# Softmax sums divided out behind the product with V instead of ahead of it, and the low parts of q and k made on VectorE

## The chip, the cores and the metric

The kernel runs on one core of one Trainium2 chip. The metric is the device time in microseconds (us) from the first to the last instruction of one execution; lower is better. PE is TensorE, DVE is VectorE, ACT is ScalarE, POOL is GpSimd and SP is SyncE, which issues the DMAs here.

## The reference, cut to what matters

```python
def _attn_ref(q, k, v, w1, b1, w2):          # B=2, H=8, S=576, D=64, hidden 32
    scores = scale * np.matmul(q, k.transpose(0, 1, 3, 2))
    x = (psi_rel / psi_i)[..., None]         # log distances, S x S
    h = np.maximum(x @ w1 + b1, 0.0)
    bias = h @ w2
    scores = scores + bias.transpose(2, 0, 1)[None, :, :, :]
    scores = scores - np.max(scores, axis=-1, keepdims=True)
    attn = np.exp(scores)
    attn = attn / (np.sum(attn, axis=-1, keepdims=True) + 1e-09)
    return np.matmul(attn, v)
...
x = attn_out.transpose(0, 2, 1, 3).reshape(B * S, H * D)
x = _moe_ref(x=x, **moe_kwargs)              # 4 experts, 512 -> 1024 -> 512
return _moe2_ref(x=x, **moe2_kwargs)         # 8 experts and a Sinkhorn gate
```

All is float32. Attention is the first fifth of the time, the two expert layers are the rest.

## The kernel before

**Attention** goes over 36 units. A unit is 128 rows of queries (a tile of one batch, or the last 64 rows of both batches together: the first four units), for one pair of heads. The loop `for k in range(U + 3)` is a pipeline written out by hand: each engine runs its instructions in the order in which the loop emits them, and waits for the others where data or a buffer is missing. Iteration k holds, in this order:

- `emit_S(k)`, PE: scores of both heads, 8 products in fp32r (16 in the first four units). q and k are each split into a high part that fp32r holds exactly and a low part: `qa` and `qb` (`prep_q`, L246 and L247), and two halves of `kk` (`k_hi`, L222 or L224, and `k_lo`, L228). Behind the second head's scores follows `emit_tail(k-2)`, a transpose of the last 64 columns of both heads (L391), which uses free columns of the same PSUM tile.
- `emit_max(k)`, DVE, L358: scores plus bias into SBUF (`s`) with the maximum, one instruction a head. Its bias tile `bt` comes through DRAM, from `emit_bias_out`.
- `emit_exp(k)`, ACT, L371: exponentials in place, with row sums into `stat`.
- `emit_T(k-2)`, PE, L401: eight transposes of `s` into the PSUM tiles `tp`, and `emit_evac`, which copies them to SBUF as `at` (L410 on ACT, L408 on DVE).
- `groups(1)`: four products of a small network for the bias table (PE, L294), copied out by ACT (L320) and written to DRAM. `hids(1)`, `hids(1)`, `hids(2)`: the hidden layer of the next group, DVE, L280, in a ring of six places; the last two wait for the group's products. The 36 groups end in iteration 25.
- `emit_recip(k)`: row sums plus 1e-9 (L377) and their reciprocals (L378), on DVE; `emit_norm(k)`: POOL multiplies `s` by them, 128x576 for each head (L383).
- `emit_P(k-3)`, PE, L427: the product of `at` and V into PSUM (`po`), transposed, heads on the partitions and rows of queries along the free dimension; `emit_x(k-3)`, ACT, L439: `po` to SBUF as `rows`.
- For every new tile and pair, `prep_q` two tiles ahead: a cast on DVE, a subtraction on POOL. In iterations 16 to 18 and from 23 on a part of `pieces(1, 0)` as well (operands of the first expert layer: L108 to L115 on DVE, L99 on ACT, L100 on DVE and POOL), and from 28 on parts of the first weights (L161 on ACT, L162 on POOL).

**The experts** follow: PE products in split precision (L651, L730), with DVE, ACT and POOL around them.

Of the kernel before, what the change touches and what calls it, by code (L numbers as in the profile page):

```python
# [9 lines left out]
F32 = mybir.dt.float32  # L10
# [18 lines left out]
# token tiles of 128: tile t of batch b; the last 64 rows of both batches share one  # L29
TILES = [(0, 0), (0, 1), (4, 0), (1, 0), (1, 1), (2, 0), (2, 1), (3, 0), (3, 1)]  # L30
# a chunk of tokens falls into two halves of n tokens: its tiles, n, and the pieces that
# pair the halves: (tile, column) of the first and of the second, width, place in the half
# [4 lines left out]
# Winograd's form of Strassen's product for first layers: operands of the tokens and of the weights  # L37
# [3 lines left out]
# columns of the packed constants  # L41
# [7 lines left out]
def attn_moe_moe(ctx: ExitStack, tc: tile.TileContext, pack, keep, rel, qT, kT, vT, w, out):  # L49
# [27 lines left out]
    # the tokens, 128 to a tile: as rows for sums over experts, or transposed for products  # L77
# [12 lines left out]
    def pieces(layer, c):  # L90
        """Work that makes the operands of a chunk, in parts."""
        n = CHUNKS[c][1]
        for i in XA:
            X[layer, c, i] = xpools[c].tile([128, 2, 2, n], F32R, tag=f"x{c}{i}", name=f"x{layer}{c}{i}")

        def split(i, src, o, w, lo):
            x = X[layer, c, i]
            hi = x[:, 0, :, o:o + w]
            sc.activation(out=hi, in_=src, func=AF.Copy)  # L99
            lo.tensor_tensor(out=x[:, 1, :, o:o + w], in0=src, in1=hi.bitcast(F32), op=ALU.subtract)  # L100

        def piece(k1, c1, k2, c2, w, o):
            h1, h2 = col_tile(k1)[:, :, c1:c1 + w], col_tile(k2)[:, :, c2:c2 + w]
            a11, a12, a21, a22 = h1[:, 0:2], h1[:, 2:4], h2[:, 0:2], h2[:, 2:4]
            t1, t2 = (g1.tile([128, 2, 128], F32, tag=f"t{i}", name=f"t{i}_{layer}{k1}")[:, :, 0:w] for i in range(2))

            def part1(eng, other):
                eng.tensor_tensor(out=t1, in0=a21, in1=a22, op=ALU.add)  # L108
                eng.tensor_tensor(out=a21, in0=a11, in1=a21, op=ALU.subtract)
                eng.tensor_tensor(out=t2, in0=t1, in1=a11, op=ALU.subtract)  # L110
                split("A11", a11, o, w, other)

            def part2(eng, other):
                split("A12", a12, o, w, eng)
                eng.tensor_tensor(out=a12, in0=a12, in1=t2, op=ALU.subtract)  # L115
                split("A22", a22, o, w, other)
                split("S1", t1, o, w, eng)

            def part3(eng, other):
                split("S2", t2, o, w, eng)  # L120
                split("S3", a21, o, w, eng)
                split("S4", a12, o, w, eng)

            return [part1, part2, part3]

        return [piece(*x) for x in CHUNKS[c][2]]

    # ------------------------------------------------------------ weights
# [14 lines left out]
    def split_raw(m, add, lo):  # L143
        """Work that makes a granule of what was loaded, in parts."""
# [8 lines left out]
        # B11, B12, B21, B22 -> B11, T1, B21, B22 and T2, T3, -T4  # L153
# [21 lines left out]
    # ------------------------------------------------------------ attention  # L175
    def attention(moe):
# [73 lines left out]
        def load_bias(t, p):  # L250
            # the second head's last 64 columns come before its others, next to the first head's
# [3 lines left out]
            # row i of the tile, column j: distance j - (i0 + i), kept at S - 1 + j - (i0 + i)  # L255
# [9 lines left out]
        # the space of the first weights serves until they come  # L265
# [62 lines left out]
        scps, sm, at_t, po = {}, {}, {}, {}  # L328
        stat = {}

        def emit_S(u):
            t, p, b = units[u]
            for h in range(2):
# [15 lines left out]
                if h == 1 and 2 <= u and made < NGR:  # L349
                    emit_tail(u - 2, sm[u - 2], o[:, 1, 288:416])  # L350
# [25 lines left out]
        def emit_recip(u):  # L376
            ve.tensor_scalar(stat[u][:, 4:6], stat[u][:, 2:4], 1e-9, None, op0=ALU.add)  # L377
            ve.reciprocal(stat[u][:, 6:8], stat[u][:, 4:6])  # L378

        def emit_norm(u):  # L380
            for h in range(2):
                s = sm[u][:, S * h:S * h + S]
                gp.tensor_tensor(  # L383
                    out=s, in0=s, in1=stat[u][:, 6 + h:7 + h].to_broadcast([128, S]), op=ALU.mult
                )
            stat.pop(u)
# [3 lines left out]
        def emit_tail(u, s, tail):  # L390
            pe.transpose(tail, s[:, 512:640], ident)  # L391
            tps[u, 2] = tail

        def emit_T(u):
            s = sm.pop(u)
            if (u, 2) not in tps:
                emit_tail(u, s, pt.tile([128, 1, 512], F32, tag="bps", name=f"tl{u}", bufs=1)[:, 0, 0:128])
            for h in range(2):
                o = pt.tile([128, 4, 128], F32, tag=f"tp{h}", name=f"tp{u}{h}", bufs=1)
                for j in range(4):  # L400
                    pe.transpose(o[:, j, :], s[:, 640 * h + 128 * j:640 * h + 128 * j + 128], ident)  # L401
                tps[u, h] = o
        def emit_evac(u, h, eng):
            o = tps.pop((u, h))
            shape = [128, 4, 128] if h < 2 else [128, 128]
# [7 lines left out]
        def emit_P(u):  # L413
# [4 lines left out]
            a = [at_t.pop((u, h)) for h in range(3)]  # L418
            for bb in [b] if t < 4 else [0, 1]:
                n = 128 if t < 4 else 64  # L420
                c0, i0 = (128 * bb, 0) if t < 4 else (64 * bb, 64 * bb)
                for j in range(5):
                    for h in range(2):
                        r = slice(0, 128) if j < 4 else slice(64 * h, 64 * h + 64)
                        col = (2 * bb + h) * D
                        rhs = a[h][:, j, i0:i0 + n] if j < 4 else a[2][r, i0:i0 + n]
# [8 lines left out]
        def emit_x(u):  # L435
            t, p, b = units[u]
            if t == 4 or b == 1:
                n = 2 if t < 4 else 1
                sc.activation(  # L439
                    out=rows[t][:, :, 128 * p:128 * p + 128],  # L440
                    in_=po.pop((t, p))[:, 0:128 * n].rearrange("p (b c) -> p b c", b=n),
                    func=AF.Copy,
                )

        # ---- emission
        kq = [(p, b) for p in range(4) for b in range(2)]
        # the clock of the tensor engine rises with work: some ahead of the first data
# [36 lines left out]
        for g in range(FIRST):  # L484
            hids(2, (1,))
            groups(1)
            if g == 0:
                load_k(*kq[2])
                prep_q(*tps_[0], gp)
                prep_k(*kq[0], ve, gp)  # L490
            if g == 1:
                load_k(*kq[3])
                prep_k(*kq[1], ve, gp)
                prep_q(*tps_[1], gp)
            if g == 3:
# [5 lines left out]
                prep_k(*kq[2], sc, gp)  # L501
            if g == 4:
                k_hi(*kq[3], sc)
                k_lo(*kq[3], gp)
# [7 lines left out]
        for k in range(U + 3):  # L512
            first = False
            if k < U:
# [5 lines left out]
                emit_max(k)  # L520
            elif k == U:
                st_sc.close()
# [29 lines left out]
            if k < U:  # L552
                emit_recip(k)
                emit_norm(k)
# [4 lines left out]
            # loads and preparation ahead  # L559
            if first:  # L560
                if ti + 2 < len(tps_):
                    prep_q(*tps_[ti + 2], gp)
# [5 lines left out]
            if k == 0:  # L568
                k_lo(*kq[4], gp)
# [4 lines left out]
            if k == 1:  # L574
                k_hi(*kq[6], sc)
                k_lo(*kq[6], gp)
# [28 lines left out]
    # ------------------------------------------------------------ experts  # L605
    class Moe:
# [25 lines left out]
        def L1(self, n):  # L632
            """Products of step n's first layer, each with what follows it."""
# [83 lines left out]
        def L2(self, n):  # L717
            """Products of step n's second layer, a tile of tokens each."""
# [56 lines left out]
        # ---- between the layers  # L775
# [101 lines left out]
        def prefetch(self, n, lo=None):  # L877
            k = self.next_split
            m = k - SLOTS
            # granule m was used last in step 2 * NP * expert + NP + pair  # L880
# [50 lines left out]
def _layouts(q, k, v, w1, b1, w2, moe_domain_probs, moe_w1, moe_w2, moe2_w_gate, moe2_w1, moe2_w2):  # L931
# [23 lines left out]
    def granules(wa, wb):  # L955
        # quadrants of a pair of first-layer columns: (rows' half, column) 00, 01, 10, 11
# [26 lines left out]
```

## Time and profile before

| what | value |
|---|---|
| median of 3 runs | 1461.72 us (1458.29 to 1463.8) |
| the profiled execution, first to last instruction | 1461.6 us |
| busy share of that span: PE / DVE / ACT / POOL | 94% / 60% / 35% / 34% |
| mean granted clock of PE, of full speed | 0.972 |
| start of the first scores (PE) | 26.1 us |
| last unit's `emit_max` | 262 us |

The span is the time of one execution under the profiler; it stands within the spread of the three runs. A busy share is an average over stages with different limits, so the stages are read one by one.

### The profile page before, as it was taken

The page shows a single profiled execution, that of the slowest core. Times are in us where ns is not written, and L with a number is a line of the kernel's source. Part 1 is how long each engine was busy: PE and PEld are TensorE (multiplying, and loading weights), DVE is VectorE, ACT ScalarE, POOL GpSimd, SP SyncE. Part 2 cuts the span into 40 slices and gives each one's busy share as a digit, 9 for nine tenths or more (in the row PEclk, how much of TensorE's full clock was granted, in tenths as well). Part 3 has the DMA queues.
Part 4 walks back from the last instruction along what each step waited for, and adds up shares of the span by engine and source line. Part 5 has one row for each costly group of instructions (what it writes and reads, how often), then busy time and mean ns, then how long its engine had stood idle before and what let it go on. Part 6 is the DMA issues. An engine that isn't in the chain of part 4 may idle for free.

```text
span 1461.6 us, 22030 instructions
## 1 busy us (share of the span) xinstructions
PE 1378.2 (94%) x8567; PEld 1190.5 (81%) x8567; DVE 870.3 (60%) x1786; ACT 505.5 (35%) x1202; POOL 492.2 (34%) x413
## 2 busy tenths in 40 slices
PE   6788876899999999999998999999999999999998
PEld 3466555778989989888887889899898898988987
DVE  6888888765646547367458356455463554635633
ACT  4466654432313224134323123132241331422311
POOL 3555446332505216024215026053160440612600
PEclk8899999999999999999999999999999999999999
DMA  6845442010201102002001002011020120200110
GB/s 192 261 140 151 116 122 61 30 58 30 87 1 58 58 1 94 23 14 74 30 29 59 29 30 87 1 59 58 1 88 29 41 76 1 87 30 30 58 37 29
DMA packets 38648, 89.88 MB, mean 61 GB/s; under 512 B 8848, under 2 KB 11664, under 8 KB 38544
## 3 DMA queue, kind: packets, MB, share of 16 engines
q1 hardware_dynamic: 38544, 88.48, 19.5%
q8 instruction: 67, 1.10, 0.3%
q14 instruction: 37, 0.30, 0.1%
HBM read 75.22 MB, written 13.25 MB: 61 GB/s over the span
## 4 chain that ended last, share of the span: by engine, by line
PE 77%; DVE 13%; ACT 5%; issue 3%; DMA 2%; SPq 0%; POOL 0%; DVEq 0%
PE y L730 40%; PE B L651 15%; PE C L651 10%; PE A L651 10%; ACT s L371 3%; DVE hids L280 2%; DVE s L358 2%; ACT at L410 1%; DVE qa L246 1%; DVE x10S L100 1%; PE bps L294 1%; DMA kr<-in_kT 1%; DVE t L110 1%; PE sc L340 1%; PE po L427 0%
## 5 line engine op out<-in xcount | busy, mean ns | idle before, releaser
L730 PE MATMUL y<-gb,h 128*128 128x512 f32 x2592 | 720.2, 398 | 0.0
L730 PEld LDWEIGHTS y<-gb,h 128*128 128x128 f32 x2592 | 455.7, 190 | 57.7 <-issue 0.2
L162 POOL TENSOR_TENSOR gb<-rawb,gb 128x512 fp32r<-128x512 f32 x94 | 125.4, 1346 | 645.1 <-ACT gb L161 645.1
L659 DVE TENSOR_TENSOR u<-B,s 128x320 f32<-128x320 f32 (+1 forms) x192 | 87.6, 456 | 311.3 <-PE B L651 311.2
L662 ACT ACTIVATE h<-c 128x320 fp32r<-128x320 f32 (+1 forms) x288 | 119.6, 439 | 402.8 <-DVE c L659 401.7
L665 DVE SCALAR_TENSOR_TENSOR h<-c,h 128x320 fp32r<-128x320 f32 (+1 forms) x288 | 167.4, 598 | 48.5 <-ACT h L662 43.7
L659 DVE TENSOR_TENSOR c<-C,u 128x320 f32<-128x320 f32 (+1 forms) x192 | 87.4, 455 | 63.3 <-PE C L651 59.8
L162 POOL TENSOR_TENSOR ga<-rawa,ga 128x512 fp32r<-128x512 f32 x94 | 121.1, 1306 | 2.8 <-ACT ga L161 2.8
L383 POOL TENSOR_TENSOR s<-s,stat 128x576 f32<-128x576 f32 x72 | 85.0, 1201 | 106.2 <-DVE stat L378 42.0
L162 POOL TENSOR_TENSOR ga<-wt,ga 128x512 fp32r<-128x512 f32 x94 | 105.0, 1135 | 43.6 <-ACT ga L161 26.1
L673 ACT ACTIVATE s<-A 128x320 f32<-128x320 f32 (+1 forms) x96 | 39.4, 411 | 180.8 <-PE A L651 180.7
L659 DVE TENSOR_TENSOR c<-B,s 128x320 f32<-128x320 f32 (+1 forms) x96 | 43.9, 457 | 81.9 <-PE B L651 80.5
L662 ACT ACTIVATE h<-A 128x320 fp32r<-128x320 f32 (+1 forms) x96 | 38.9, 406 | 151.0 <-PE A L651 151.0
L280 DVE TENSOR_SCALAR hids<-T,b1psi 128x528 f32<-128x528 f32 (+17 forms) x137 | 87.4, 672 | 5.7 <-PE bps L294 5.6
L161 ACT ACTIVATE gb<-rawb 128x512 fp32r<-128x512 f32 x96 | 60.0, 626 | 74.4 <-DMA rawb<-in_w 74.4
L371 ACT ACTIVATE s<-s,stat 128x576 f32<-128x576 f32 x72 | 55.4, 770 | 86.2 <-DVE stat L358 86.2
L340 PE MATMUL sc<-kk,qa 128*128 128x288 f32 x160 | 51.5, 340 | 22.6 <-DVE stat L358 17.2
L651 PE MATMUL C<-x20S,ga 128*128 128x320 f32 x384 | 67.4, 311 | 0.0
L651 PE MATMUL A<-x20A,ga 128*128 128x320 f32 x384 | 66.8, 309 | 0.0
L651 PEld LDWEIGHTS C<-x20S,ga 128*128 128x128 f32 x384 | 62.1, 190 | 5.8
L651 PE MATMUL B<-x20S,ga 128*128 128x320 f32 x384 | 66.5, 308 | 0.0
L651 PEld LDWEIGHTS A<-x20A,ga 128*128 128x128 f32 x384 | 61.6, 189 | 5.7
(157 smaller groups left out, 2104.3 us busy)
## 6 DMA issues: line engine op xcount, KB each, us to landing
rawa<-in_w SPq DMA_DIRECT2D x48, 512.0 KB, 4.1
rawb<-in_w SPq DMA_DIRECT2D x48, 512.0 KB, 4.9
bd<-bsts SPq DMA_DIRECT2D x36, 295.5 KB, 3.4
bt<-bd SPq DMA_DIRECT2D x16, 512.0 KB, 4.4
qr<-in_qT SPq DMA_DIRECT2D x20, 256.0 KB, 3.6
kr<-in_kT SPq DMA_DIRECT2D x8, 576.0 KB, 6.2
bt<-bd SPq DMA_DIRECT2D x8, 256.0 KB, 4.8
V<-in_vT SPq DMA_DIRECT2D x4, 512.0 KB, 6.1
```

What stands on the lines that cost most here:

```text
L161: sc.activation(out=z(0), in_=src, func=AF.Copy)
L162: lo.tensor_tensor(out=z(1), in0=src, in1=z(0).bitcast(F32), op=ALU.subtract)
L280: ve.tensor_scalar(x[:, 0:n], T[:, 0:n], b1psi[:, tt:tt + 1], 0.0, op0=ALU.add, op1=ALU.max)
L340: pe.matmul(out=o[:, j, 0:288], lhsT=qq[t, p][:, 2 * bb + h, :], rhs=kk[p, bb][:, h, 288 * j:288 * j + 288], start=n == 0, stop=n == last,)
L371: sc.activation(out=s, in_=s, func=AF.Exp, scale=-1.0, bias=stat[u][:, h:h + 1], accum_out=stat[u][:, 2 + h:3 + h],)
L383: gp.tensor_tensor(out=s, in0=s, in1=stat[u][:, 6 + h:7 + h].to_broadcast([128, S]), op=ALU.mult)
L651: pe.matmul(out=ban[o], lhsT=a, rhs=x[:, z, k, :], start=not more and i == 0, stop=i == 5, skip_group_check=more,)
L659: ve.tensor_tensor(out=t[o], in0=ban[a], in1=t[b], op=ALU.add)
L662: sc.activation(out=h[f][:, 0, half, :], in_=src, func=AF.Relu)
L665: ve.scalar_tensor_tensor(out=h[f][:, 1, half, :], in0=src, scalar=0.0, in1=h[f][:, 0, half, :].bitcast(F32), op0=ALU.max, op1=ALU.subtract,)
L673: sc.activation(out=t["s1"], in_=ban["A"], func=AF.Copy)
L730: pe.matmul(out=self.y[t], lhsT=a, rhs=x, start=g == 0 and f == 0 and i == 0, stop=g == NP - 1 and f == 1 and i == 2,)
```

## The change

Row sums are no longer multiplied into `s` by POOL. The exponentials are transposed and multiplied by V as they are. The addition of 1e-9 moves from DVE to POOL (`emit_recip`), the reciprocal stays on DVE, one iteration later (`emit_recip2(k-1)`, right behind `emit_max(k)`). Since `po` is transposed, its scale is needed along the free dimension: `emit_tail` makes it with one more small product a head, whose stationary operand is the reciprocal column repeated 64 times and whose moving operand is the identity, so that each of the 64 output partitions holds all 128 reciprocals. It lies beside the transposed tail in PSUM, and the tail's copy to SBUF takes both (256 columns in place of 128). `emit_x` becomes a multiplication on DVE, for each unit, of `po` with that copy, in place of a copy on ACT for every two units. The subtractions of `prep_q` and of six of the eight `k_lo` move from POOL to DVE. Comments were taken out as well.

```diff
@@ emit_S @@
-                    emit_tail(u - 2, sm[u - 2], o[:, 1, 288:416])
+                    emit_tail(u - 2, sm[u - 2], o[:, :, 288:416])
@@ -374,27 +374,29 @@
         def emit_recip(u):
-            ve.tensor_scalar(stat[u][:, 4:6], stat[u][:, 2:4], 1e-9, None, op0=ALU.add)
+            gp.tensor_scalar(stat[u][:, 4:6], stat[u][:, 2:4], 1e-9, None, op0=ALU.add)
+
+        def emit_recip2(u):
             ve.reciprocal(stat[u][:, 6:8], stat[u][:, 4:6])
 
-        def emit_norm(u):
+        tps = {}
+
+        def emit_tail(u, s, o):
+
+            pe.transpose(o[:, 1, :], s[:, 512:640], ident)
+            st = stat.pop(u)
             for h in range(2):
-                s = sm[u][:, S * h:S * h + S]
-                gp.tensor_tensor(
-                    out=s, in0=s, in1=stat[u][:, 6 + h:7 + h].to_broadcast([128, S]), op=ALU.mult
+                pe.matmul(
+                    out=o[64 * h:64 * h + 64, 0, :], lhsT=st[:, 6 + h:7 + h].to_broadcast([128, 64]),
+                    rhs=ident, start=True, stop=True,
                 )
-            stat.pop(u)
-
-        tps = {}
-
-        def emit_tail(u, s, tail):
-            pe.transpose(tail, s[:, 512:640], ident)
-            tps[u, 2] = tail
+            tps[u, 2] = o
...
@@ emit_evac @@
-            shape = [128, 4, 128] if h < 2 else [128, 128]
+            shape = [128, 4 if h < 2 else 2, 128]
@@ emit_P @@
+            rc[u] = a[2][:, 0, :]
...
-                        rhs = a[h][:, j, i0:i0 + n] if j < 4 else a[2][r, i0:i0 + n]
+                        rhs = a[h][:, j, i0:i0 + n] if j < 4 else a[2][r, 1, i0:i0 + n]
@@ -434,17 +437,14 @@
         def emit_x(u):
             t, p, b = units[u]
-            if t == 4 or b == 1:
-                n = 2 if t < 4 else 1
-                sc.activation(
-                    out=rows[t][:, :, 128 * p:128 * p + 128],
-                    in_=po.pop((t, p))[:, 0:128 * n].rearrange("p (b c) -> p b c", b=n),
-                    func=AF.Copy,
-                )
+            ve.tensor_tensor(
+                out=rows[t][:, b, 128 * p:128 * p + 128],
+                in0=po[t, p][:, 128 * b:128 * b + 128], in1=rc.pop(u), op=ALU.mult,
+            )
@@ attention, ahead of the loop and in it @@
-                prep_q(*tps_[0], gp)
-                prep_k(*kq[0], ve, gp)
+                prep_q(*tps_[0], ve)
+                prep_k(*kq[0], ve, ve)
...
-                k_lo(*kq[3], gp)
+                k_lo(*kq[3], ve)
...
                 emit_S(k)
                 emit_max(k)
+                if k > 0:
+                    emit_recip2(k - 1)
...
                 emit_recip(k)
-                emit_norm(k)
...
-                    prep_q(*tps_[ti + 2], gp)
+                    prep_q(*tps_[ti + 2], ve)
...
-                k_lo(*kq[4], gp)
+                k_lo(*kq[4], ve)
```

On DVE, one whole iteration of the middle of attention (from one `emit_max` to the next; `s` and `stat` are the unit's scores and sums, `sc` its PSUM tile, `hids` the hidden layer, `qa` the cast of q) stands before as

```order
L358 ISA s_1048,stat_1047<-sc_1036,bt_901 128x576
L358 ISA stat_1047 128x1
L358 ISA s_1048,stat_1047<-sc_1041,bt_901 128x576
L358 ISA stat_1047 128x1
L280 TENSOR_SCALAR hids<-T,b1psi 128x304
L408 COPY at_1076<-sc_1041 128x128
L280 TENSOR_SCALAR hids<-T,b1psi 128x304
L377 TENSOR_SCALAR stat_1047<-stat_1047 128x2
L378 RECIPROCAL stat_1047<-stat_1047 128x2
L280 TENSOR_SCALAR hids<-T,b1psi 128x304 x2
L246 CAST qa_1096<-qr_840 128x512
```

and the same iteration of the changed kernel as

```order
L358 ISA s_1047,stat_1046<-sc_1033,bt_897 128x576
L358 ISA stat_1046 128x1
L358 ISA s_1047,stat_1046<-sc_1038,bt_897 128x576
L358 ISA stat_1046 128x1
L380 RECIPROCAL stat_983<-stat_983 128x2
L280 TENSOR_SCALAR hids<-T,b1psi 128x304
L410 COPY at_1076<-sc_1038 128x256
L280 TENSOR_SCALAR hids<-T,b1psi 128x304 x3
L440 TENSOR_TENSOR rows_76<-po,at_1013 128x128
L246 CAST qa_1093<-qr_835 128x512
L247 TENSOR_TENSOR qb_1094<-qr_835,qa_1093 128x512
```

The addition has gone, the reciprocal is that of the unit before (`stat_983`), and the product of `po` and the subtraction for `qb` are new.

On PE, an early unit of the changed kernel, from its last score product to the first product with V (`kept` holds the identity):

```order
L340 MATMUL sc_617<-kk_160,qb_499 128x288
L386 MATMUL sc_617<-kept,s_450 128x128
L389 MATMUL sc_617<-kept,stat_449 64x128 x2
L403 MATMUL tp_631<-kept,s_450 128x128 x4
L403 MATMUL tp_636<-kept,s_450 128x128 x4
L294 MATMUL bps_644<-hids,w2n 32x416 x4
L430 MATMUL po<-at_547,V_101 64x64
```

The row with `stat_449` is new: two small products between the tail's transpose and the others, which need the reciprocals of the unit two back.

## Rows read from the trace of the kernel before

**Rows 1.** Windows: stretch, length, busy us (instructions) of PE, PEld, DVE, ACT, POOL, clock, DMA.

```profile
72.00:146.00 74.00, 66.30 (x682) 47.27 (x679) 64.65 (x158) 47.65 (x113) 39.96 (x34) 0.95 0.52 149
146.00:216.00 70.00, 54.66 (x457) 38.22 (x459) 61.70 (x137) 40.27 (x105) 34.81 (x32) 0.93 0.44 124
216.00:262.00 46.00, 32.21 (x277) 25.41 (x273) 39.01 (x78) 23.26 (x69) 27.87 (x27) 0.92 0.17 49
```

**Rows 2.** Waits, 84 to 195 us: who waited for whom, us in total, times, longest.

```profile
ACT s L371 <- DVE stat L358: 38.6, 18, 4.1
...
DVE stat L377 <- ACT s L371: 12.0, 19, 0.7
```

**Rows 3.** Timeline near 124 us: start, duration, engine, line, operation, idle before.

```profile
123.74 0.39 DVE L280 TENSOR_SCALAR hids<-T,b1psi 128x336 f32<-128x336 f32 x1
...
125.60 1.59 DVE L280 TENSOR_SCALAR hids<-T,b1psi 128x336 f32<-128x336 f32 x2
125.85 2.34 POOL L383 TENSOR_TENSOR s<-s,stat 128x576 f32<-128x576 f32 x2 [2.03 <-PE tp L401]
```

**Rows 4.** Timeline: two casts of q, and POOL's next instruction beside the second.

```profile
131.84 1.37 DVE L246 CAST qa<-qr 128x512 fp32r<-128x512 f32 x1
...
206.19 0.41 DVE L246 CAST qa<-qr 128x512 fp32r<-128x512 f32 x1
...
206.44 2.31 POOL L383 TENSOR_TENSOR s<-s,stat 128x576 f32<-128x576 f32 x2 [3.74 <-ACT rows L439]
```

**Rows 5.** Groups by line, 0 to 310 us: count, busy us, mean ns, idle before; POOL and DVE.

```profile
L383 POOL TENSOR_TENSOR s<-s,stat 128x576 f32<-128x576 f32 x72 | 85.0, 1201 | 106.2 <-DVE stat L378 42.0 <-ACT rows L439 15.9 <-PE tp L401 15.6
L247 POOL TENSOR_TENSOR qb<-qr,qa 128x512 fp32r<-128x512 f32 x20 | 25.7, 1285 | 12.8 <-DVE qa L246 11.9 <-ACT kk L222 0.4 <-PE tp L401 0.4
...
L228 DVE TENSOR_TENSOR kk<-kr,kk 64x1152 fp32r<-64x1152 f32 x2 | 5.2, 2603 | 0.1
...
L100 DVE TENSOR_TENSOR x10S<-rows,x10S 128x128 fp32r<-128x128 f32 x10 | 9.9, 1025 | 0.0
```

**Rows 6.** Timeline behind attention: a DVE subtraction, and POOL's next instruction.

```profile
273.59 0.68 DVE L162 TENSOR_TENSOR gb<-rawb,gb 128x512 fp32r<-128x512 f32 x1
...
286.38 1.34 POOL L162 TENSOR_TENSOR gb<-rawb,gb 128x512 fp32r<-128x512 f32 x1 [18.68 <-ACT gb L161]
```

**Rows 7.** Timeline: DVE's copies out of PSUM, 128 and 512 columns.

```profile
124.04 0.28 DVE L408 COPY at<-sc 128x128 f32<-128x128 f32 x1
...
204.33 0.68 DVE L408 COPY at<-tp 128x512 f32<-128x512 f32 x1
```

**Rows 8.** Timeline: PE from one unit's scores to the next unit's.

```profile
129.44 0.40 PE L340 MATMUL sc<-kk,qa 128*128 128x288 f32 x1
...
131.48 0.66 PE L401 MATMUL tp<-kept,s 128*128 128x128 f32 x4 [0.18 <-ACT at L410]
...
132.80 1.46 PE L427 MATMUL po<-at,V 128*64 128x128 f32 x20
...
134.19 0.40 PE L340 MATMUL sc<-kk,qa 128*128 128x288 f32 x1
```

**Rows 9.** Groups by line, 0 to 310 us: ACT's exponentials, bias table and copies.

```profile
L371 ACT ACTIVATE s<-s,stat 128x576 f32<-128x576 f32 x72 | 55.4, 770 | 86.2 <-DVE stat L358 86.2
L320 ACT ACTIVATE bsts<-bps,cst 128x64 f32<-128x64 f32 (+35 forms) x72 | 36.2, 502 | 25.6 <-PE bps L294 17.4 <-DMA bd<-bsts 3.7 <-DMA V<-in_vT 3.3
L410 ACT ACTIVATE at<-tp 128x512 f32<-128x512 f32 x59 | 34.3, 582 | 0.5 <-PE tp L401 0.5
```

**Rows 10.** Timeline: first `emit_max` instruction of units 0, 4, 17, 28 and 35.

```profile
32.78 0.76 DVE L358 CUSTOM_DVE_ANT_0 s<-sc,bt 128x576 f32<-128x576 f32 x1 [2.59 <-DMA bt<-bd]
...
71.50 0.76 DVE L358 CUSTOM_DVE_ANT_0 s<-sc,bt 128x576 f32<-128x576 f32 x1 [1.42 <-POOL qb L247]
...
145.87 0.74 DVE L358 CUSTOM_DVE_ANT_0 s<-sc,bt 128x576 f32<-128x576 f32 x1
...
215.93 0.74 DVE L358 CUSTOM_DVE_ANT_0 s<-sc,bt 128x576 f32<-128x576 f32 x1
...
261.99 0.74 DVE L358 CUSTOM_DVE_ANT_0 s<-sc,bt 128x576 f32<-128x576 f32 x1
```

More of the change, by code (lines that the diff above doesn't have):

```diff
@@ L326, in emit_bias_out @@
             )
-        scps, sm, at_t, po = {}, {}, {}, {}
+        scps, sm, at_t, po, rc = {}, {}, {}, {}, {}
         stat = {}
@@ L396, in emit_T @@
             if (u, 2) not in tps:
-                emit_tail(u, s, pt.tile([128, 1, 512], F32, tag="bps", name=f"tl{u}", bufs=1)[:, 0, 0:128])
+                o = pt.tile([128, 1, 512], F32, tag="bps", name=f"tl{u}", bufs=1)
+                emit_tail(u, s, o[:, 0, 0:256].rearrange("p (a c) -> p a c", a=2))
             for h in range(2):
@@ L488, in attention @@
                 load_k(*kq[2])
-                prep_q(*tps_[0], gp)
-                prep_k(*kq[0], ve, gp)
+                prep_q(*tps_[0], ve)
+                prep_k(*kq[0], ve, ve)
             if g == 1:
                 load_k(*kq[3])
-                prep_k(*kq[1], ve, gp)
-                prep_q(*tps_[1], gp)
+                prep_k(*kq[1], ve, ve)
+                prep_q(*tps_[1], ve)
             if g == 3:
@@ L500, in attention @@
                 load_q(*tps_[2])
-                prep_k(*kq[2], sc, gp)
+                prep_k(*kq[2], sc, ve)
             if g == 4:
                 k_hi(*kq[3], sc)
-                k_lo(*kq[3], gp)
+                k_lo(*kq[3], ve)
             if g == 5:
@@ L520, in attention @@
                 emit_max(k)
+                if k > 0:
+                    emit_recip2(k - 1)
             elif k == U:
+                emit_recip2(k - 1)
                 st_sc.close()
@@ L575, in attention @@
                 k_hi(*kq[6], sc)
-                k_lo(*kq[6], gp)
+                k_lo(*kq[6], ve)
                 k_hi(*kq[7], sc)
```

## The prediction

> **What bounds the kernel now.** I read the page first: PE is busy for 94% of the span and its slices are full wherever the experts run. The change touches nothing there, so all it can move lies in attention, which I read by stages. The windows show that DVE, not PE, is the fuller engine in the middle and at the end of attention: 64.65 us of 74, 61.70 of 70 and 39.01 of 46, while PE falls to 54.66 of 70 and 32.21 of 46 [rows 1]. PE leads only in the first of the three, with 66.30.
>
> The waits name the link: ACT stood 38.6 us in 111 for `emit_max` on DVE, and DVE itself stood 12.0 us for the exponentials before it could add 1e-9, in 19 waits [rows 2]. A busy engine is not yet a working one. The timeline shows one `hids` instruction of 336 columns at 0.39 us, and two us later a pair of the same at 1.59, when POOL multiplies `s` [rows 3]. A cast of q takes 1.37 us in one place and 0.41 in another, where POOL had been idle for 3.74 us and starts only after most of the cast [rows 4]. So DVE is slow where POOL runs, and POOL runs the 72 multiplications that are removed, 85.0 us in all [rows 5].
>
> The Trainium skill (SBUF — State Buffer, section "SBUF: two separate sides") calls the ports that DVE and POOL share an exclusive lock, held for a whole instruction. The trace agrees, with 0.39 against about 0.80 a piece for `hids`. By that rule the subtractions that move to DVE cost their undisturbed time; by the disturbed rows [rows 5] the same 26 would be dearer by 20 x 0.61 + 6 x 1.07 = 19 us.
>
> The time per unit, from the starts of `emit_max` [rows 10]: units 4 to 17 take 74.37 us, 5.72 each; 17 to 28 take 70.06, 6.37 each; 28 to 35 take 46.06, 6.58 each.
>
> **The change, part by part.** I make the sum for a middle unit first, on DVE.
> - Removed: the slow half of `hids`, 1.59 - 2 x 0.39 = 0.81 us [rows 3]; in every second unit the slow cast, 1.37 - 0.41 = 0.96, so 0.48 a unit [rows 4]; the wait for the exponentials, 12.0 / 19 = 0.63 [rows 2], since the reciprocal is now taken a whole iteration later, when the sums are long there. The addition's own time goes too; I don't count it.
> - Added: `emit_x`, 128 columns out of PSUM, like the copy of 0.28; the tail's copy with 256 columns, by the two copies of 128 and 512, 0.40 x 128 / 384 = 0.13 more [rows 7]; `qb` in every second unit. With POOL silent (its next instruction comes 13 us later, after 18.68 us of idleness) a subtraction of 512 columns takes 0.68 [rows 6], so 0.34 a unit.
> - DVE would then need 5.72 - 0.81 - 0.48 - 0.63 + 0.28 + 0.13 + 0.34 = 4.55 us a unit.
>
> On PE the fastest unit of before took 134.19 - 129.44 = 4.75 us, of which 0.18 was a wait for ACT [rows 8]. The two products with the reciprocals are not in the trace. The nearest are the products with V: 20 records, two for each of ten products, in 1.46 us, 0.07 a record [rows 8], so four records cost 0.29. Bounds: nothing, if they lie beside others in other columns of the array, and 0.66, what four transposes of as many columns take [rows 8]. I take 0.29, the row they are nearest to: PE needs 4.75 - 0.18 + 0.29 = 4.86. PE takes over from DVE.
>
> A new wait comes with it. `emit_x` on DVE waits for the product with V, which is the last thing PE does in an iteration; the casts, `qb` and the next `emit_max` are queued behind it, and ACT waits for that. Link by link over two units: `emit_x` 0.28, cast 0.41, `qb` 0.68, `emit_max` of two heads 2 x 0.74 [rows 4, 6, 7, 10], then on ACT the second exponential 0.77, two bias copies 1.00 and the second copy 0.58, with the first exponential and first copy, 0.77 + 0.58, partly beside `emit_max` (I count all but the 0.74 of its second head) [rows 9], then on PE the last transposes and bias products 131.48 to 132.80 = 1.32 and the product with V 1.46 [rows 8]. That is 8.59 us, and with nine hand-overs of an estimated 0.15 each 9.9 us for two units, 4.97 each. It binds as tightly as PE does. I take 5.0 us a unit.
>
> The addition on POOL costs nothing: between the sums and the reciprocal lies a whole iteration less `emit_max`, some 3 us. ACT loses the copies of `po`, which it does beside others.
>
> By stages:
> - Units 4 to 17: 13 x 5.0 = 65.0 instead of 74.37, -9.4.
> - Units 17 to 28: seven of the eleven carry a part of `pieces(1, 0)`, three subtractions on DVE, 1.03 us each now [rows 5]; undisturbed they can't be below the 0.28 of a small copy [rows 7]. POOL still makes some low parts there, so I take 0.45 each, 1.35 a unit: DVE needs 4.55 + 1.35 = 5.9 where `hids` still run and less where they have ended; 5.6 on the mean. 7 x 5.6 + 4 x 5.0 = 59.2 instead of 70.06, -10.9.
> - Units 28 to 35: no `hids` and no bias products, but `pieces`, the copy of half of `tp` on DVE (0.68) and the first weights on ACT and POOL. I take 5.2: 36.4 instead of 46.06, -9.7. Bounds of both pieces stages: PE's 4.86, and the 5.9 of DVE.
> - Start to unit 4 (71.5 us): the first `emit_max` waits 2.59 us for the bias tile by DMA [rows 10], so faster `hids` ahead of it help little. Of the six `k_lo` that come to DVE, the ones for the third, fourth and seventh tile need ACT's copy of k, which stands behind the bias copies; the `hids` queued behind them on DVE wait too, and PE's bias products for those. Each costs at most 0.68 x 1152 / 512 = 1.5 us undisturbed [rows 6], where the two already on DVE go from 2.60 [rows 5] to that. Gain and loss nearly meet; the slow `hids` and casts of units 2 and 3 remain. I take -4, between 0 and -8.
> - Behind unit 35: the last transposes no longer wait for POOL's 2.3 us [rows 4]; -1, between 0 and -3.
>
> Sum: -9.4 - 10.9 - 9.7 - 4 - 1 = -35 us. The profiled execution is 1461.6 us, the median of the runs 1461.72, so both lead to **1427 us**.
>
> **The rivals.**
> - *More* (PE alone sets the pace, the loop over `emit_x` is slack, the products with the reciprocals are nearly free): 31 units at 4.86, 150.7 instead of 190.5, -39.8, with -8 and -3 at the ends, -51: 1411 us. For it: PE reached 4.75 even beside POOL. Against it: DVE's 5.9 in the units with pieces. Chance 0.13.
> - *Less* (the loop over `emit_x` binds harder): with hand-overs of 0.30 instead of 0.15 it is 11.3 us, 5.6 a unit, and 6.0 where pieces stand in it: -1.6, -6 and -4, with -2 at the start, -14: 1448 us. For it: every link is in-order and none can be overtaken. Against: the loop spans two units and the fast ones of before had such hand-overs too. Chance 0.19.
> - *Slower*: the slow `hids` and casts are not POOL's doing, and stay. Then DVE, the fuller engine, only gains the 0.63 of the wait and pays 0.28 + 0.13 + 1.29 / 2 = 1.06 (`qb` at its present 1285 ns [rows 5]): +0.43 a unit, 13 us in 31 units, and six `k_lo` at 2.6 us, 15.6, half of them exposed: 1461.6 + 21 = 1483 us. It decides if less than 0.12 us a unit (0.28 + 0.13 + 0.34 - 0.63) of the slowness is POOL's. Against it stand the paired rows [rows 3, 4]. Chance 0.05. The Trainium skill (Perfetto Trace Analysis, section "Optimizing Scalar/DVE Operations") advises moving work off a saturated DVE, to GpSimd too, which is the reverse of this edit; the same passage adds that between these two it might not help, as they share a port, and the pairs above agree with the second half.
> - *No change*, within 7 us, if the DMAs behind the bias tiles (`emit_bias_out` to `load_bias`) hold the units at their present times. Against: after the first units `emit_max` hardly waits for one [rows 10]. Chance 0.03.
>
> **How the numbers follow.** The likeliest case, -26 to -44 us, has 0.60; the predicted time is its middle. A measurement of this kernel tells about 0.5%, 7.3 us, from no change. Faster takes the likeliest, *more* and *less*: 0.92; same 0.03; slower 0.05. The range reaches to *more* and nearly all of *less*: 1411 to 1447. What is left out is about 0.15: the end of *less*, no change, slower, and a sliver beyond *more*.
>
> **What the changed profile would show.** Right: `hids` near 0.4 us a piece instead of 0.67 and casts near 0.41; DVE without a wait for the exponentials, but with one for the product with V at `emit_x`; units 4 to 17 about 5.0 us apart, with PE busy for over 92% there; no unit with pieces above 6; the reciprocals' products near 0.3 us a unit; `qb` on DVE near 0.68; the experts as long as before. Wrong: casts that stay over 1 us although POOL is idle (the port is not the cause); units at 5.5 and more with DVE waiting long at `emit_x` (*less*); a first `emit_max` well behind 33 us (the moved `k_lo` hold the start); reciprocals that wait for POOL's addition.

## The result

The changed kernel takes 1419.43 us (median, 1415.2 to 1420.91) beside 1460.01 us for the kernel before on the same chip: the ratio is 0.9715, with a 95% interval of 0.9693 to 0.9738. The profiled execution spans 1418.1 us, 43.5 less than that of before. The prediction was 1427 us, in a range of 1411 to 1447.

The windows of the changed kernel answer to [rows 1]; the columns are the same.

```profile
72.00:146.00 74.00, 74.00 (x795) 52.54 (x793) 59.95 (x190) 52.48 (x123) 5.00 (x17) 1.00 0.54 154
146.00:216.00 70.00, 68.89 (x665) 49.63 (x662) 60.08 (x182) 51.24 (x137) 13.89 (x26) 1.00 0.48 137
216.00:262.00 46.00, 43.51 (x326) 36.37 (x324) 35.81 (x72) 23.80 (x60) 15.69 (x16) 1.00 0.21 67
```

PE (first busy figure) is now without a gap from 72 to 146 us and nearly so behind; POOL (fifth) fell from 39.96 to 5.00 us in the first of the three stretches of [rows 1]. PE's granted clock is 1.00 where it was 0.92 to 0.95.

The groups by line on DVE and POOL, 0 to 270 us, answer to [rows 5]; columns are count, busy us, mean ns, idle before. `hids` and the cast stood before as

```profile
L280 DVE TENSOR_SCALAR hids<-T,b1psi 128x528 f32<-128x528 f32 (+17 forms) x137 | 87.4, 672 | 5.7 <-PE bps L294 5.6
...
L246 DVE CAST qa<-qr 128x512 fp32r<-128x512 f32 x20 | 20.2, 1010 | 0.3 <-DMA qr<-in_qT 0.3
```

and the changed kernel has

```profile
L280 DVE TENSOR_SCALAR hids<-T,b1psi 128x528 f32<-128x528 f32 (+17 forms) x137 | 53.8, 438 | 2.9 <-PE bps L294 2.5
...
L247 DVE TENSOR_TENSOR qb<-qr,qa 128x512 fp32r<-128x512 f32 x20 | 14.1, 705 | 0.7
L228 DVE TENSOR_TENSOR kk<-kr,kk 64x1152 fp32r<-64x1152 f32 x8 | 10.8, 1355 | 8.6 <-ACT kk L222 8.5
L440 DVE TENSOR_TENSOR rows<-po,at 128x128 f32<-128x128 f32 x36 | 10.4, 289 | 16.3 <-PE po L430 15.5 <-ACT at L412 0.8
L410 DVE COPY at<-sc 128x256 f32<-128x256 f32 x24 | 10.0, 417 | 0.0
...
L246 DVE CAST qa<-qr 128x512 fp32r<-128x512 f32 x20 | 8.4, 418 | 0.0
...
L100 DVE TENSOR_TENSOR x10S<-rows,x10S 128x128 fp32r<-128x128 f32 x10 | 2.4, 284 | 0.0
...
L377 POOL TENSOR_SCALAR stat<-stat 128x2 f32<-128x2 f32 x36 | 11.0, 307 | 189.0 <-ACT s L371 178.1 <-PE bps L294 9.4 <-issue 1.5
```

The durations came out close to the undisturbed rows: the cast 418 ns, `qb` 705, the multiplication at L440 289, the tail's copy 417, and the subtractions of `pieces` fell from 1025 ns to 284. What DVE waits for now stands in the idle columns: 15.5 us for the product with V at L440, and 8.5 us for ACT's copies of k at L228.

The first `emit_max` of units 0, 4, 17, 28 and 35 answers to [rows 10].

```profile
35.39 0.76 DVE L358 CUSTOM_DVE_ANT_0 s<-sc,bt 128x576 f32<-128x576 f32 x1 [2.21 <-PE sc L340]
...
71.38 0.75 DVE L358 CUSTOM_DVE_ANT_0 s<-sc,bt 128x576 f32<-128x576 f32 x1
...
136.82 0.75 DVE L358 CUSTOM_DVE_ANT_0 s<-sc,bt 128x576 f32<-128x576 f32 x1
...
191.36 0.74 DVE L358 CUSTOM_DVE_ANT_0 s<-sc,bt 128x576 f32<-128x576 f32 x1
...
220.92 0.75 DVE L358 CUSTOM_DVE_ANT_0 s<-sc,bt 128x576 f32<-128x576 f32 x1
```

So the 43.5 us fall as follows, by differences of such starts: start to unit 4, 0.1; units 4 to 17, 8.9; 17 to 28, 15.5; 28 to 35, 16.5; behind unit 35, 2.4. Of the last one 1.6 us come and go between executions: the same program takes 1197.2 us behind unit 35 here and 1198.8 in another execution.

### The profile page after: what moved, and what is told of

It is laid out like the page before. It is cut to its first block, busy times and chain, and to the rows that moved or that the text cites. A ratio compares the mean times of both kernels' runs of the same rounds, so it can differ in the third digit from the quotient of the medians.

```text
span 1418.1 us, 22243 instructions
## 1 busy us (share of the span) xinstructions
PE 1373.2 (97%) x8711; PEld 1185.6 (84%) x8711; DVE 820.9 (58%) x1812; ACT 502.5 (35%) x1182; POOL 377.1 (27%) x351
## 4 chain that ended last, share of the span: by engine, by line
PE 88%; DVE 7%; ACT 2%; issue 1%; DMA 1%; SPq 0%; DVEq 0%; ACTq 0%
PE y L732 40%; PE B L653 16%; PE C L653 10%; PE A L653 10%; PE po L430 3%; PE sc L340 3%; PE bps L294 2%; PE tp L403 2%; ACT s L371 1%; PE sc L389 1%; DVE wt L157 0%; DMA kr<-in_kT 0%; ACT at L412 0%; DVE kk L228 0%; DVE h L667 0%
## 5 line engine op out<-in xcount | busy, mean ns | idle before, releaser
L161 ACT ACTIVATE gb<-rawb 128x512 fp32r<-128x512 f32 x96 | 60.0, 626 | 70.4 <-DMA rawb<-in_w 70.4
L653 PEld LDWEIGHTS B<-x20S,ga 128*128 128x128 f32 x384 | 61.4, 188 | 5.7
L294 PE MATMUL bps<-hids,w2n 128*32 128x264 f32 (+17 forms) x352 | 45.1, 538 | 21.4 <-DVE hids L280 17.4
L377 POOL TENSOR_SCALAR stat<-stat 128x2 f32<-128x2 f32 x36 | 11.0, 307 | 189.0 <-ACT s L371 178.1
```

The lines of the kernel that those rows point to most:

```text
L161: sc.activation(out=z(0), in_=src, func=AF.Copy)
L294: pe.matmul(out=o[32 * q:32 * q + 32, j, 0:n], lhsT=w2n, rhs=hid[g, q][:, n * j:n * j + n], start=True, stop=True,)
L653: pe.matmul(out=ban[o], lhsT=a, rhs=x[:, z, k, :], start=not more and i == 0, stop=i == 5, skip_group_check=more,)
```

## The experiments

The table has the same starts for every run, from its profiled execution (us), and the time per unit in the three stages. Each ratio is against the kernel before on the same chip. The start differs from one execution to the next: unit 4 came at 71.4 and 70.7 us in two executions of the changed kernel, and at 69.3 and 68.8 in two versions (`emit_x` later, products twice) that have the same low parts there and take nothing away from the first units. So differences of up to some 2.6 us at unit 4 show nothing by themselves.

| run | median | ratio, 95% interval | unit 0 | unit 4 | unit 35 | 4 to 17 | 17 to 28 | 28 to 35 |
|---|---|---|---|---|---|---|---|---|
| before | 1460 to 1463 | 1 | 32.8 | 71.5 | 262.0 | 5.72 | 6.37 | 6.58 |
| changed | 1419.4 | 0.9715, 0.9693 to 0.9738 | 35.4 | 71.4 | 220.9 | 5.03 | 4.96 | 4.22 |
| low parts only | 1468.3 | 1.0051, 1.0036 to 1.0065 | 37.0 | 75.0 | 270.5 | 5.95 | 6.42 | 6.79 |
| sums only | 1426.3 | 0.9764, 0.9746 to 0.9782 | 32.5 | 68.2 | 223.5 | 5.10 | 5.05 | 4.77 |
| k's low parts on POOL | 1417.7 | 0.9707, 0.9690 to 0.9725 | 33.2 | 69.3 | 218.9 | 5.03 | 4.96 | 4.22 |
| POOL beside | 1442.9 | 0.9878, 0.9860 to 0.9897 | 35.9 | 73.8 | 241.9 | 5.25 | 5.92 | 4.96 |
| `emit_x` later | 1418.1 | 0.9696, 0.9675 to 0.9718 | 35.1 | 69.3 | 219.3 | 5.01 | 4.95 | 4.34 |
| products twice | 1420.1 | 0.9717, 0.9692 to 0.9741 | 36.4 | 68.8 | 223.4 | 5.25 | 5.11 | 4.31 |
| one product, by DVE | 1420.2 | 0.9712, 0.9689 to 0.9735 | 34.6 | 70.1 | 220.1 | 4.76 | 5.05 | 4.64 |
| k's low parts later | 1418.4 | 0.9701, 0.9681 to 0.9721 | 31.1 | 68.5 | 218.1 | 5.04 | 4.96 | 4.22 |
| changed, again | 1420.9 | 0.9706, 0.9679 to 0.9732 | 35.8 | 70.7 | 220.2 | 5.03 | 4.96 | 4.22 |
| POOL as before | 1442.8 | 0.9868, 0.9846 to 0.9891 | 32.0 | 70.4 | 241.7 | 5.23 | 5.96 | 5.39 |
| reciprocal at once | 1424.8 | 0.9759, 0.9733 to 0.9785 | 36.7 | 73.0 | 230.4 | 5.03 | 5.07 | 5.18 |
| one product by POOL, k later | 1409.1 | 0.9643, 0.9619 to 0.9666 | 31.2 | 68.4 | 213.4 | 4.75 | 4.88 | 4.22 |

**Low parts only.** The kernel before, with this alone:

```diff
-                prep_q(*tps_[0], gp)
-                prep_k(*kq[0], ve, gp)
+                prep_q(*tps_[0], ve)
+                prep_k(*kq[0], ve, ve)
...
-                    prep_q(*tps_[ti + 2], gp)
+                    prep_q(*tps_[ti + 2], ve)
```

> The kernel before with one part of the change alone: the low parts of q and of six tiles of k on VectorE; POOL still multiplies the exponentials by the reciprocals. Theory (POOL's instructions stretch DVE's, and taking the 72 multiplications off POOL is what frees DVE): DVE gets 0.34 us a unit more and loses only the disturbance by the low parts; hids and the cast stay slow beside the multiplications. 1462 to 1475 us, no gain; units 4 to 17 at 5.6 to 6.0 us. Rival (the gain comes from the low parts leaving POOL): most of the 42 us are here already, 1425 to 1435 us.

1468.3 us, 0.5% slower: the rival fell. `hids` stayed slow at 607 ns and the cast at 1080. Unit 35 comes 8.5 us later than before; 3.5 of these are there at unit 4, so a part of the loss lies in the start, where DVE now waits 7.9 us for ACT's copies of k (L228).

**Sums only.** The changed kernel with those lines as they were before.

> The changed kernel with all low parts of q and k back on POOL, so only the row sums are handled anew. Theory: POOL runs 1.3 us in every second unit, beside a cast or hids; DVE then needs about 4.7 us a unit and PE's 4.8 still sets the pace, so the middle stays as in the changed kernel; the first emit_max comes at about 32 us instead of 35.4, since no subtraction on DVE waits for ACT there. 1413 to 1421 us. Rival (the moved low parts carry a part of the gain): 1428 us or more, with units 4 to 17 over 5.3 us.

1426.3 us, between the two expectations: the low parts are worth some 7 us of the 41 once the multiplications are gone. The first `emit_max` came at 32.5 us, as expected, so there the move of the low parts costs 3 us; it gains where it was expected to gain nothing, above all in the last units (4.77 against 4.22 us).

**K's low parts on POOL.** The changed kernel with `prep_k(..., gp)` and `k_lo(..., gp)` alone undone.

> The changed kernel with the six low parts of k back on POOL, and q's low parts on DVE. Theory (at the start hids stand on DVE behind subtractions that wait for ACT's copies of k): the first emit_max comes 2 to 3 us earlier, at 32 to 33.5 us, unit 4 at 68 to 70 us, and the whole at 1415 to 1418 us. Rival (the start is bound by the DMAs of the bias tiles and of V): the first units move, unit 4 doesn't, 1419 us.

Unit 0 came at 33.2 us, and the units behind 4 take what they take in the changed kernel. That the start gained at unit 4 (69.3 us) isn't shown, since it lies within the differences of the starts, and the medians can't tell the two kernels. Beside the run before it, this one says which low parts carry the 7 us: with k's back on POOL the time stays at 1417.7, with q's back as well it is 1426.3. The gain is that of q's 20 subtractions; moving k's brought nothing that can be measured.

**POOL beside.** Work for POOL that nobody waits for:

```diff
                 emit_recip(k)
+                for _ in range(2):
+                    gp.tensor_tensor(out=dm, in0=T, in1=b1psi[:, 0:1].to_broadcast([128, S]), op=ALU.mult)
```

> The changed kernel with two more instructions on POOL in each of the 36 units, at the place where the multiplications stood: the table T of distances (128x576) times a column, into a tile that nothing reads. They have the old ones' shape, and nobody waits for them. Theory (the port: a running POOL instruction stretches DVE's): hids and casts are slow again, DVE needs 5.5 to 5.9 us a unit and sets the pace; 1436 to 1452 us. Rival (the gain came from taking POOL's multiplication out of the chain between exponentials and transposes, and DVE's slow rows were only a symptom): 1419 us, within 4 us.

1442.9 us, 23 more than the changed kernel and within the theory's range, though the units came to 5.5 us and more only between 17 and 28 (5.92). The groups by line show where; `dm` is the tile that nothing reads.

```profile
L281 DVE TENSOR_SCALAR hids<-T,b1psi 128x528 f32<-128x528 f32 (+17 forms) x137 | 68.8, 550 | 2.2 <-PE bps L295 2.0
...
L248 DVE TENSOR_TENSOR qb<-qr,qa 128x512 fp32r<-128x512 f32 x20 | 19.8, 989 | 0.7
L247 DVE CAST qa<-qr 128x512 fp32r<-128x512 f32 x20 | 12.7, 634 | 0.0
...
L559 POOL TENSOR_TENSOR dm<-T,b1psi 128x576 f32<-128x576 f32 x72 | 86.8, 1205 | 5.7
```

`hids` went from 438 to 550 ns, the cast from 418 to 634, `qb` from 705 to 989, though no data or buffer ties them to POOL's instruction. That POOL's instructions stretch DVE's is shown, and that it costs time. By what mechanism isn't: the rows show the stretch, not that a port is held for a whole instruction.

**POOL as before.** Both: the low parts back on POOL, and the two instructions a unit beside.

> The changed kernel with POOL loaded as before: the low parts of q and k back on it, and two instructions a unit of the old multiplications' shape that nobody waits for. What is left of the change is only the order: nobody waits for POOL's multiplication, DVE doesn't wait for the exponentials. Theory A (the port is all of it): 1455 to 1465 us. Theory B (the port is the larger part, and DVE's wait of 0.63 us a unit for the exponentials with the chain over POOL the rest): 1443 to 1452 us.

1442.8 us, at the edge of theory B. With as much work on POOL as before, and a little more, the kernel keeps 20 us of the gain. That doesn't make the stretching half of it, for the added instructions start earlier in an iteration than the old multiplications, which waited for the reciprocals, and DVE's rows show that they disturb less:

```profile
L281 DVE TENSOR_SCALAR hids<-T,b1psi 128x528 f32<-128x528 f32 (+17 forms) x137 | 78.0, 615 | 3.9 <-PE bps L295 3.8
...
L247 DVE CAST qa<-qr 128x512 fp32r<-128x512 f32 x20 | 12.9, 647 | 0.0
```

Beside their 53.8 and 8.4 us in the changed kernel, `hids` and casts were busy for 24.2 and 4.5 us more here, and for 33.6 and 11.8 more before: less than two thirds of the stretching came back. So the stretching is likely more than half of the gain and the order of the waits less; where the two part, this run doesn't show.

**Reciprocal at once.** Addition and reciprocal on DVE in the unit's own iteration:

```diff
-            gp.tensor_scalar(stat[u][:, 4:6], stat[u][:, 2:4], 1e-9, None, op0=ALU.add)
-
-        def emit_recip2(u):
+            ve.tensor_scalar(stat[u][:, 4:6], stat[u][:, 2:4], 1e-9, None, op0=ALU.add)
...
-                if k > 0:
-                    emit_recip2(k - 1)
```

> The changed kernel with addition and reciprocal back on DVE in the unit's own iteration, so that DVE waits for the exponentials again; POOL does none of it. Theory (the wait is worth what it was in the trace of before, 0.63 us a unit on DVE, and makes up most of the 20 us that remain when POOL is as loaded as before): where DVE is as full as PE, in the units with pieces and behind them, 0.4 to 0.8 us a unit more, in units 4 to 17 at most 0.3; 1426 to 1436 us. Rival (with POOL out of the way DVE has room for the wait everywhere): 1420 us within 3, and the 20 us come from POOL's multiplication leaving the chain to the transposes.

1424.8 us, just short of the theory's range and 4 to 5 us above the two medians of the changed kernel. Its five executions lie apart, three at 1424 to 1425 us and two at 1431.6 and 1431.7; the profiled one is of the two, and from unit 4 to 35 it takes 157.5 us against 149.5. The wait is back on DVE, between 72 and 200 us and in units 28 to 35:

```profile
DVE stat L377 <- ACT s L371: 12.2, 25, 0.9
```

```profile
DVE stat L377 <- ACT s L371: 6.3, 7, 0.9
```

Yet units 4 to 17 keep 5.03 us: PE hides it there. It costs in units 28 to 35, 5.18 us against 4.22, about the 0.90 a unit that DVE waits. So the wait, with the addition's own 0.17 us a unit on DVE, is worth 4 to 8 of the 20 us. The rest is argued to be POOL's multiplication leaving the chain to the transposes, and the part of the stretching that "POOL as before" lacked; no run isolates the two.

**`emit_x` later.** `emit_x(k - 4)` right behind `emit_recip2(k - 1)` in place of `emit_x(k - 3)` behind `emit_P(k - 3)`, and three places for the tail's copy.

> The changed kernel with emit_x one iteration later, right behind the next emit_max, where the product with V has long ended, and a third place for the tail's copy; nothing on DVE waits for that product any more. Theory (PE's own work sets the pace in the middle, busy for 74.0 of 74 us there): nothing, 1419 us within 4; in the last units, where PE has gaps, at most 3 us less. Rival (the loop over emit_x that the prediction weighed as equal binds): 0.15 to 0.3 us a unit less in 31 units, 1409 to 1414 us.

1418.1 us, and no stage's units got shorter by more than 0.03 us (28 to 35 took 4.34 in place of 4.22). The rival fell: the loop over `emit_x` has slack.

**Products twice.**

```diff
-            for h in range(2):
+            for h in [0, 1, 0, 1]:
```

> The changed kernel with the two products of reciprocals and identity made twice for each unit, into the same place, so the result stays. Theory (PE sets the pace wherever bias products run): four more records at 0.07 to 0.09 us, 0.3 to 0.37 us a unit in the 30 units from unit 4 on in which PE has no gaps, so 1427 to 1432 us, and units 4 to 17 at 5.3 to 5.4 us. Rival (PE is busy but not what binds, and the products lie in gaps): 1419 us within 3.

Units 4 to 17 take 5.25 us in place of 5.03, and from unit 4 to 35 it is 154.6 us against 149.5. A row of PE's timeline in this run and one in the changed kernel give the price of the second pair:

```profile
105.72 0.66 PE L389 MATMUL sc<-kept,stat 128*64 128x128 f32 x8
```

```profile
106.77 0.44 PE L389 MATMUL sc<-kept,stat 128*64 128x128 f32 x4
```

Four records more, 0.22 us more, and 0.22 us more a unit: what PE is given there, the unit takes. The theory's place was right and its price of 0.3 to 0.37 us for a second pair too high. What the first pair costs, this run doesn't show; the part on the prediction reads it from other rows. The median, 1420.1 us, doesn't show the addition: the start of this execution was 2.6 us earlier than in the first one of the changed kernel, and the intervals are 3.5 us to either side.

**One product, by DVE.** The reciprocal written 64 times side by side for each head (128 columns), and one product for both heads.

> The changed kernel with the reciprocals written by DVE 64 times side by side, for both heads (128 columns), so that one product with the identity makes both heads' scales: two records a unit fewer on PE, a longer reciprocal on DVE. Theory (PE sets the pace): 0.15 to 0.2 us a unit less in some 30 units, 1413 to 1416 us. Rival (PE's pace is not what binds, or DVE's longer reciprocal delays the tail's copy as much): 1419 us within 3.

Units 4 to 17 fell to 4.76 us, but 28 to 35 rose to 4.64, and the median stayed, as the rival had it. The cause is one row:

```profile
L381 DVE RECIPROCAL rb<-stat 128x128 f32<-128x128 f32 x36 | 34.1, 948 | 0.3 <-POOL stat L377 0.3
```

DVE pays 948 ns for 128 columns in place of 159 for two, and in units 28 to 35, where it is busy for 30.92 of 32.50 us in this run, this comes back.

**K's low parts later.**

```diff
-                prep_k(*kq[2], sc, ve)
+                k_hi(*kq[2], sc)
...
-                k_lo(*kq[3], ve)
...
             hids(2)
+        k_lo(*kq[2], ve)
+        k_lo(*kq[3], ve)
```

> The changed kernel with two of the six low parts of k (the third and fourth tile) still on DVE, but behind all the hids of the start, when ACT's copies are long there, in place of ahead of two sets of hids. Theory (7.3 us of DVE waits for ACT's copies of k held the start): the first emit_max at 30 to 33 us in place of 35.4, unit 4 at 67 to 69.5 in place of 71.4, the whole at 1415 to 1417.5 us. Rival (the start is bound by the DMAs of the bias tiles): the first emit_max at 33 or later, unit 4 as it is, 1419 us.

The first `emit_max` came 4.3 us earlier and waits for the DMA of the bias tile, as before the change:

```profile
31.07 0.76 DVE L358 CUSTOM_DVE_ANT_0 s<-sc,bt 128x576 f32<-128x576 f32 x1 [3.42 <-DMA bt<-bd]
```

Unit 4 came at 68.5 us, 2.9 earlier than in the one execution and 0.3 before the earliest of the starts with the low parts ahead, so how much of the gain at unit 0 is left there stays open. Its median of 1418.4 us can't be told from the changed kernel's.

**Changed, again**, beside the last version on one chip.

> The changed kernel as it is, beside the next two on one chip: 1417 to 1421 us by every theory; its first units show how far the start differs from one execution to the next (unit 4 was at 68.8 to 71.4 us in kernels whose starts are the same).

1420.9 us. Its units agree with the first execution to the hundredth; its unit 4 came 0.7 us earlier.

**One product by POOL, k later.** The last edit, and for the first 22 units POOL copies the reciprocals to 128 columns, so that one product serves both heads:

```diff
             ve.reciprocal(stat[u][:, 6:8], stat[u][:, 4:6])
+            if u < 22:
+                rb[u] = atb.tile([128, 2, 64], F32, tag="rb", name=f"rb{u}", bufs=2)
+                gp.tensor_copy(rb[u], stat[u][:, 6:8].unsqueeze(2).to_broadcast([128, 2, 64]))
...
+            if u in rb:
+                pe.matmul(
+                    out=o[:, 0, :], lhsT=rb.pop(u).rearrange("p h c -> p (h c)"),
+                    rhs=ident, start=True, stop=True,
+                )
```

> The changed kernel with the two late low parts of k behind the hids of the start, and one product for both heads' scales in the first 22 units, whose 128 columns POOL copies from the reciprocals (DVE's reciprocal stays at two columns). Theory (PE sets the pace in the middle): 0.2 us a unit less in units 4 to 23, -4, and -2 to -3 at the start; 1411 to 1415 us, units 4 to 17 at 4.75 to 4.85 us. Rival (POOL's copy stretches DVE's instructions or delays the product): units at 5.0 or more, 1416 to 1420 us.

1409.1 us, 0.9643 (0.9619 to 0.9666) where the changed kernel beside it has 0.9706 (0.9679 to 0.9732): the intervals don't meet, and it lies below the theory's range. Units 4 to 17 take 4.75 us, as expected; from unit 4 to 35 it is 4.5 us less than in the execution beside it, and unit 4 comes 2.3 us earlier, which is within what starts differ by. The rest lies behind unit 35 (1191.3 us against 1198.8; the other runs have 1195 to 1200), where the program is the same, so the edit doesn't explain it. PE's granted clock is higher there, 1.00 against 0.97 in the first 60 us and 0.98 against 0.96 from 400 to 600 us behind unit 35 (0.98 against 0.99 from 200 to 400); why, no run shows. What the edit is shown to gain are the 4.5 us.

## Why the prediction held, point by point

- **What bounds attention.** DVE's stretched instructions before, PE after. Shown: `hids` and casts took the durations that the paired rows gave [rows 3, 4], POOL's work put back beside them stretched them again, and in units 4 to 17 the 0.22 us added on PE were 0.22 us a unit. Behind unit 28 PE alone doesn't set the pace: there the same addition took a unit from 4.22 to 4.31 us only, and DVE's returned wait to 5.18.
- **Units 4 to 17:** 5.0 us forecast, 5.03 measured; -9.4 against -8.9. But of the two reasons given for 5.0, PE's own work and the loop over `emit_x`, only the first holds: the loop was counted as equally tight, and taking the wait away changed nothing. PE's 4.86 stood near the truth (a unit of the changed kernel took PE 4.81, from 105.39 to 110.20 us), but by luck: two of its terms were wrong by the same amount, as the next point shows. And the step from 4.86 to 5.0, close to the stage's mean, was taken for the loop, which doesn't bind.
- **The products:** 0.29 us a unit forecast, 0.52 measured. PE's timeline shows it, from the tail's transpose to the first bias product: before, in the changed kernel, and with one product for both heads (by POOL).

```profile
76.56 0.27 PE L391 MATMUL sc<-kept,s 128*128 128x128 f32 x1
76.67 1.04 PE L401 MATMUL tp<-kept,s 128*128 128x128 f32 x8
77.63 0.88 PE L294 MATMUL bps<-hids,w2n 128*32 128x400 f32 x8
```

```profile
106.57 0.27 PE L386 MATMUL sc<-kept,s 128*128 128x128 f32 x1
...
108.16 0.72 PE L294 MATMUL bps<-hids,w2n 128*32 128x304 f32 x8
```

```profile
106.21 0.27 PE L389 MATMUL sc<-kept,s 128*128 128x128 f32 x1
...
107.51 0.72 PE L294 MATMUL bps<-hids,w2n 128*32 128x304 f32 x8
```

   These are 1.07, 1.59 and 1.30 us: the pair costs 0.52, one product for both heads 0.23, and a second pair 0.22. The forecast took the pair for four records like those of the product with V. Its other PE term was too high: it took 0.18 us, the idle time, off the unit of [rows 8] as that unit's wait for ACT. Between the starts of its first transposes and its bias products lay 1.37 us, where a unit without the wait takes 0.96 (76.67 to 77.63):

```profile
130.70 0.60 PE L401 MATMUL tp<-kept,s 128*128 128x128 f32 x4
...
132.07 0.80 PE L294 MATMUL bps<-hids,w2n 128*32 128x352 f32 x8
```

   So the wait was worth 0.41 us. The two errors, 0.23 each, cancel.
- **Units 17 to 28 and 28 to 35:** 5.6 (with pieces) and 5.2 us forecast, 4.96 and 4.22 measured, 15.5 and 16.5 us gained against 10.9 and 9.7. Two terms were mis-sized. The subtraction of `pieces` on DVE was taken at 0.45 us for POOL's remaining low parts; it took 0.284, the undisturbed value that the prediction had as its bound. And DVE's 4.55 us without pieces were too many: it was busy for 59.95 of 74 us at 5.03 a unit, 4.1 each. So PE is the fuller engine in both stages (PE is the first busy figure, DVE the third):

```profile
136.82:191.36 54.54, 54.28 (x525) 37.44 (x524) 46.61 (x142) 39.14 (x100) 6.46 (x16) 1.00 0.57 163
191.36:220.92 29.56, 28.71 (x281) 22.40 (x279) 25.30 (x79) 22.88 (x65) 10.30 (x16) 1.00 0.27 82
```

   And the lower bound of 4.86 us held bias products, which are gone behind unit 28: a unit took 4.22. One sign of being right failed: the `emit_max` of unit 25, behind a unit with pieces, came 6.44 us after that of 24, above the 6 of the forecast.
- **Start to unit 4:** 4 us forecast, 0.1 measured. The term that failed is "Gain and loss nearly meet": two of the moved `k_lo` waited 7.3 us for ACT's copies of k, with `hids` and with them PE behind them, and the first `emit_max` came at 35.4 us, not at 32.8. The waits up to the first `emit_max` (us in total, times, longest) show the link and who stands behind it, before:

```profile
PE bps L294 <- DVE hids L280: 6.8, 5, 2.1
```

   and in the changed kernel:

```profile
PE bps L294 <- DVE hids L280: 14.1, 4, 4.1
...
DVE kk L228 <- ACT kk L222: 7.3, 2, 3.9
```

   The prediction had named that wait and its sign of being wrong, but no price for it. Emitting the two later brought the first `emit_max` back to 31.1 us. How large the error is stays open: the four executions named above the table had unit 4 at 68.8 to 71.4 us, a gain of 0.1 to 2.7 on the one start of before that was traced, and short of 4 in all of them.
- **The slower rival** (slow `hids` not POOL's doing) fell with the 438 ns and the added POOL work. **The addition on POOL** cost nothing: DVE has no wait for it in the changed kernel.
- **The sum** fell 8.5 us short of the 43.5. It forecast 11.4 us too little in the two stages from unit 17 to 35 and 1.4 too little behind them, 3.9 too much at the start and 0.5 too much in units 4 to 17. That it came as near as it did is in part these opposite signs.

## What to carry to other kernels

When an engine's instruction takes two lengths in one trace, look at what the neighbour does beside the longer one: work on POOL that nobody seems to wait for may be paid by DVE, and moving it to DVE can be cheaper than leaving it, as it was for q's low parts and not for k's. An instruction that is moved to an in-order engine also brings its wait, so emit it where its operands are long there. What is saved where one engine leads must not be paid on the engine that leads in the next stage. Doing a step twice prices its repetition and not the step: the second pair of products cost 0.22 us, the first 0.52, which only the starts of the instructions around it told.

## What the runs showed of the hardware

- A DVE reciprocal of 128x128 took 948 ns and one of 128x2 159, so 6.3 ns for each further column, while a multiplication of 128x128 took 289 in all.
- POOL's addition of 128x2 took 307 ns, a multiplication of 128x576 some 1205.
- Two products of 64 output partitions each, between PE's transposes, took 0.52 us of PE's time; one product of 128 output partitions in their place took 0.23.
- PE's granted clock went from between 0.92 and 0.95 (means over the two levels of 1.2 and 2.4 GHz) to 1.00, the higher level all through, where PE became busy for 74.00 of 74 and 68.89 of 70 us instead of 66.30 and 54.66. It was 1.00 as well in units 28 to 35 of "POOL beside", with PE busy for 28.70 of 34.70 us, so PE had gaps at the higher level too. The forecast had not counted the clock; it may be a part of what the stages gained, and no run separates it.
